# An FFT layer followed by a two-matmul feed-forward layer: the opening's way from B to y is rerouted, and two A units of the second batch move into the step loop

## The chip, the cores and the metric

One kernel on one core of a Trainium2 chip. The metric is the device time of one execution in microseconds; a run's profile gives one execution seen by the hardware profiler. Engines are named as in the profile: PE (TensorE matmul), DVE (VectorE), ACT (ScalarE), POOL (GpSimd), SP (SyncE, which here only issues DMAs).

## The reference

```python
# x: (8, 3008, 256) fp32
X = rfft(x, axis=1)
Yr = Xr @ w_r - Xi @ w_i + b_r
Yi = Xr @ w_i + Xi @ w_r + b_i
Yr, Yi = shrink(Yr, 0.01), shrink(Yi, 0.01)      # sign(v) * max(|v| - lam, 0)
y = irfft(Yr + 1j * Yi, n=3008, axis=1)           # -> 24064 tokens x 256
h = y @ w_in                                      # 256 -> 2048
g = where(h > 0, h, exp(min(h, 0)) - 1)
out = g @ w_out                                   # 2048 -> 256
```

## The kernel before

**The transform.** 3008 = 47 x 64, and each of the 8 batches goes through five kinds of unit:

- A (6 units, `unit_A`): the 64-point transform over x, four sequence columns of 256 at a time; the PSUM result is copied to a bf16 tile `A` (a pair of units fills one tile), which is written to a DRAM scratch `DA`. `load_Z` reads DA back in another partition order.
- X (8 units): the second transform stage, from Z to `XT`.
- M (12 units): multiplication with the weights and the shrinking, from XT to `Y`; bias and K sums on DVE, clip and subtract on POOL.
- B (6 units, `unit_B`, v = 0 to 5): the first inverse stage, two pairs at a time, from Y to `Bz`, which is written to a DRAM scratch `DB`. `load_Bs(b, w)` reads DB back in another partition order: 96 partitions, (k, c, h), each with the eight rows 8w to 8w + 7, for w = 0 to 3, each w a quarter of the batch's output.
- y (8 units, `unit_Y`): the last inverse stage, two units for each w, from `Bs` to the bf16 tile `yT`.

**The feed-forward layer** is a loop of steps (`for i in range(n + LAG)`). A step takes 512 tokens and two of the 16 blocks of 128 hidden channels: `front_mm` (PSUM `hps`, two banks of four), ACT exp to `Et`, a clamp of Et to 0..1 (`Elu.least`, on DVE in steps 0 to 3, afterwards on POOL), DVE `gT` = max(Et - 1, hps), and two steps later `back` (PSUM `ps_o` with `w_out_r`). Eight steps finish 512 tokens. Transform units of later batches are placed into the steps, at most one per step: its matmuls stand between the two halves of `front_mm`, and its PSUM copy comes with `flush()` after the first or second exp.

**Order.** Everything is issued in the order in which the program calls it (a manual schedule). Engines and queues work in order. A planner (`units`) chooses the unit of each step; the string `FIRST` fixes it for the first 33 steps (y: batch 0; X, M, B: batch 1; "-": none).

**The opening**, before the loop, computes batch 0 up to two y units, and the six A units of batch 1 (`ahead=True`). PE is kept busy with dummy matmuls (`idle_pe`, tile `ips`). In its last part the order is: first_M (M of batch 0) interleaved with `fB(0)` to `fB(5)`; `load_Bs(0, 0)` and `(0, 1)`; six A units with `idle_pe(2)` between them; `load_Bs(0, 2)`, `(0, 3)`; `load_w_in(3)`; `load_Z(1, ...)`; y units 0 and 1.

**Weights.** w_in comes in four quarters through staging tiles (`load_w_in`; the first three use the slots of the three Et tiles) and is scaled into `w_in_s` (`scale_w_in`): quarters 0 and 1 on DVE, 2 on ACT, 3 in the step loop on DVE. x of batch 1 and w_out are loaded by POOL's DMA queue behind a small POOL copy (`gate`) that waits for Z of batch 0.

**DMA semaphores.** DMAs from SP and ACT take eight completion semaphores in turn, so a DMA waits until the one eight places earlier has landed.

Lines that the text names (numbers of the profile): L163 A matmuls; L128 and L130 PSUM copies on DVE and ACT; L175 and L177 writes of DA; L186 `load_Z`; L197 X; L214 M of batch 0; L306 Yt, an SBUF-to-SBUF load of later batches; L347 B matmuls; L365, L366 and L368 copies to Bz; L373 writes of DB; L386 `load_Bs`; L397 y; L412 dummy matmuls; L696 `load_w_in`; L779 M4; L788 and L790 `scale_w_in`; L861 front_mm; L878 exp; L883 and L885 the clamp on POOL and DVE; L895 gT; L913 back; L246, L288, L289, L293 POOL's share of M.

Of the kernel before, what the change touches and what calls it, by code (L numbers as in the profile page):

```python
# [8 lines left out]
ALU = mybir.AluOpType  # L9
AF = mybir.ActivationFunctionType  # L10
BF16 = mybir.dt.bfloat16
F32 = mybir.dt.float32
# [13 lines left out]
def kernel(  # L26
# [115 lines left out]
            f()  # L142
        after.clear()

    def unit_A(b, u, alone=False, on_dve=False, ahead=False):
        ci, uu = u // 2, u % 2
        if uu == 0:
            if ahead and ci == 1:
                A_of[b, ci] = xtp.tile([P, 3, 8, D], BF16, name="A", tag="XT")[:, 0]
            elif ahead and ci == 2:  # L150
                A_of[b, ci] = late2.tile([P, 8, D], BF16, name="A", tag="osb")
            elif alone:
                A_of[b, ci] = wk4.tile([P, 8, D], BF16, name="A", tag="Bs")
            else:
                t = "Bz" if b == 2 and ci == 2 else "A"
                A_of[b, ci] = wk2.tile([P, 8, D], BF16, name="A", tag=t)
            if ci == 0:
                DA_of[b] = dram.tile([NJ, P, D], BF16, name="DA", tag="DA")
        xt, A = xts[ci], A_of[b, ci]
        dav = DA_of[b].rearrange("j p d -> p j d")  # L160
        ps = unit_ps("aps", alone or ahead)
        for j in range(2):
            nc.tensor.matmul(  # L163
                ps[:, j, :], lhsT=M1[:],
                rhs=xt[:, 4 * uu + 2 * j : 4 * uu + 2 * j + 2, :], start=True, stop=True,
            )
        def done():
            evac(
                A[:, 4 * uu : 4 * uu + 4, :].rearrange("p n d -> p (n d)"),
                ps[:].rearrange("p a b -> p (a b)"), on_dve,  # L170
            )
            j0 = 8 * ci
            if alone:
                j0 += 4 * uu
                nc.sync.dma_start(dav[:, j0 : j0 + 4, :], A[:, 4 * uu : 4 * uu + 4, :])  # L175
            elif uu == 1:
                nc.sync.dma_start(dav[:, j0 : j0 + 8, :], A[:])  # L177

        later(alone or ahead, done)
# [151 lines left out]
    def unit_B(b, v, alone=False, on_dve=False):  # L331
        if v % 2 == 0:
            t = "A" if alone and v == 4 else "Bz"
            Bz_of[b, v // 2] = wk2.tile([P, 8, D], BF16, name=t, tag=t)
            if v == 0:
                DB_of[b] = dram.tile([K1, P, D], BF16, name="DB", tag="DB")
        Bz = Bz_of[b, v // 2]
        ps = unit_ps("bps", alone)
        psj = ps[:].rearrange("p s (q d) -> p (s q) d", d=D)
        if b < 2:  # L340
            Y = Y_of.pop((b, v))[:]
            if b == 1:
                Y = Y.rearrange("p i c d -> p i (c d)")
            for pp in range(2):
                for c in range(2):
                    for s in range(2):
                        nc.tensor.matmul(  # L347
                            ps[:, s, pp * D : pp * D + D],
                            lhsT=M3f[c][s * N2 : s * N2 + N2, 2 * v + pp, :],
                            rhs=Y[s * N2 : s * N2 + N2, pp, c * D : c * D + D],  # L350
                            start=(c == 0), stop=(c == 1),
                        )
        else:
            Yt = Yt_of.pop((b, v))
            for j in range(4):
                nc.tensor.matmul(  # L356
                    psj[:, j], lhsT=M3[:, 4 * v + j],
                    rhs=Yt[:, j % 2, j // 2 * D : j // 2 * D + D], start=True, stop=True,
                )
        def done():  # L360
            o = 4 * (v % 2)
            Bv = Bz[:, o : o + 4, :].rearrange("p (q s) d -> p s q d", s=2)
            psv = ps[:].rearrange("p s (q d) -> p s q d", d=D)
            if on_dve:
                nc.scalar.copy(Bv[:, :, 0], psv[:, :, 0])  # L365
                nc.vector.tensor_copy(Bv[:, :, 1], psv[:, :, 1])  # L366
            elif b < 2:
                nc.scalar.copy(Bv, psv)  # L368
            else:
                nc.scalar.copy(Bz[:, o : o + 4, :], psj)  # L370
            if alone or (b == 1 and v > 3):
                k0 = 4 * v
                nc.sync.dma_start(  # L373
                    DB_of[b][k0 : k0 + 4].rearrange("k p d -> p k d"), Bz[:, o : o + 4, :]
                )
            elif v % 2:
                k0 = 8 * (v // 2)
                nc.sync.dma_start(DB_of[b][k0 : k0 + 8].rearrange("k p d -> p k d"), Bz[:])

        later(alone, done)  # L380

    def load_Bs(b, w):

        Bs = wk4.tile([4 * K1, 8, D], BF16, name="Bs", tag="Bs")
        dv = DB_of[b].rearrange("k (c h m) d -> (k c h) m d", c=2, h=2)
        nc.sync.dma_start(Bs[:], dv[:, 8 * w : 8 * w + 8, :])  # L386
        Bs_of[b, w] = Bs

    def unit_Y(b, u, alone=False, on_dve=False):
        w, dt = u // 2, u % 2  # L390
# [36 lines left out]
    with tc.tile_pool(name="stagep", bufs=1) as stagep:  # L427
# [66 lines left out]
        for e in range(2):  # L494
# [5 lines left out]
            iota("", None, [[-30, NV]], base=b3, cm=-15, out=m3i[hi])  # L500
            iota("", None, [[-30, NV]], base=b3 + 480, out=m3i[mid_])
            iota("", None, [[2, NV]], base=e, out=k1t[N2 * e : N2 * e + N2])
        n2row = iota("n2row", [P, N2], [[1, N2]])
        arow = iota("arow", [P, N1], [[1, N1]], out=arow_t[:])


# [184 lines left out]
    def load_w_in(q):  # L691
# [4 lines left out]
        nc.sync.dma_start(wf[:], w_in_v[:, :, q * FQ : q * FQ + FQ])  # L696
        w_in_f.append(wf)

    def load_w_out(hh):
        hf = slice(hh * NFT // 2, (hh + 1) * NFT // 2)  # L700
        nc.gpsimd.dma_start(w_out_r[:, hf, :], w_out_v[:, hf, :])
# [15 lines left out]
        unit_B(0, v, alone=True, on_dve=on_dve)  # L717

    load_w_in(0)
    gate(Z_of[0][:, 8, 0:1])  # L720
    for ci in range(3):
        load_x(1, ci)
# [35 lines left out]
    first_M(1, 1, True)  # L758
    first_M(2, 0, False)
    fB(0)  # L760
    load_w_in(1)
    first_M(2, 1, True)
    first_M(3, 0, False)
    fB(1)
# [3 lines left out]
    first_M(4, 1, True)  # L768
    first_M(5, 0, True)
    fB(3)  # L770
    load_w_in(2)
    first_M(5, 1, True)
    let_go()
    fB(4)
    idle_pe(3)
# [2 lines left out]
    for h, w in enumerate((w40, w41)):  # L778
        nc.gpsimd.tensor_scalar(  # L779
            M4v[:, :, h], r4[0 : 2 * NR], w[0 : 2 * NR], None, ALU.mult  # L780
        )
    load_Bs(0, 0)
    load_Bs(0, 1)

    def scale_w_in(q, on_dve, f=slice(0, FQ)):
        dst = w_in_s[:, :, q * FQ + f.start : q * FQ + f.stop]
        if on_dve:
            nc.vector.tensor_scalar_mul(dst, w_in_f[q][:, :, f], 2.0 / S)  # L788
        else:
            nc.scalar.activation(dst, w_in_f[q][:, :, f], AF.Copy, scale=2.0 / S)  # L790

    scale_w_in(0, True)
    for u in range(6):
        unit_A(1, u, on_dve=bool(u % 2), ahead=True)
        if u == 1:
            scale_w_in(1, True)
        idle_pe(2)
    for w in (2, 3):
        load_Bs(0, w)
    load_w_in(3)  # L800
    scale_w_in(2, False)
    for s0, s1 in ((0, 8), (8, NS)):
        load_Z(1, s0, s1)
    idle_pe(3)
    for u in range(2):
        unit_Y(0, u, alone=True, on_dve=bool(u % 2))
    first.close()
# [148 lines left out]
    LB, YB, ZX, LEAD, XW = 6, 7, 6, 52, 2  # L956
    SHUN = ("FFX",)

    FIRST = "yy-yyXXXXXXXXyMMyMMBMMBMMBMMMMBBB"

    def due(b, w):

# [1 line left out]

    def units():

        at = {("A", 1, k): 0 for k in range(6)} | {("y", 0, k): 0 for k in range(2)}
        xat = {(2, c): s for c, s in enumerate((12, 18, 22))}
        xat |= {(3, c): PER + 1 + 3 * c for c in range(3)}
        when = lambda *u: at.get(u, 10 * n)  # L970
# [3 lines left out]
        for t in range(1, n):  # L974
# [33 lines left out]
            if t <= len(FIRST):  # L1008
                kind = FIRST[t - 1]
                b = {"y": 0, "A": 2}.get(kind, 1)  # L1010
                u = None if kind == "-" else (kind, b, count(kind, b))
            elif must:
                u = must
            elif "M" in can and was != "M" and (tight or t % NPAIR != 1):
                u = can["M"]
            elif "B" in can and not (can["B"][1] > 1 and lately[-3:] in SHUN):
                u = can["B"]
            elif "M" in can and tight:
                u = can["M"]
            else:  # L1020
                early = t < 6 or ("y" in can and can["y"][2] < 2)
                u = next((can[k] for k in ("yXA" if early else "XAy") if k in can), None)
# [8 lines left out]
    def plan():  # L1031
# [8 lines left out]
            ):  # L1040
                whole.add((b, k))
        for (kind, b, k), t in at.items():
            if t == 0:
                continue
            name = "Y" if kind == "y" else kind
            f0[t].append(put(name, b, *((k // 2, k % 2) if kind == "M" else (k,))))
            if (kind, k) == ("X", 7):
                for j in range(2):
                    mid[t + 1 + j].append((unit_D, (b, j)))
            if (kind, k) == ("B", 5):  # L1050
                f1[t + (b > 1)] += [(load_Bs, (b, w)) for w in range(4)]
            if (kind, k) == ("A", 5):
                for p in range(2 if b == 2 else 4):
                    w = 8 if p == 0 or b > 2 else 24
                    f1[t + (0, 1, 3)[min(max(b - 2, 0), 2)] * p].append((load_Z, (b, 8 * p, 8 * p + w)))
        for (b, c), t in xat.items():
# [2 lines left out]
            f1[5 + k].append((weight_sum, (k,)))  # L1059
        for c in range(2):  # L1060
            f1[24 + c].append((turn_M3, (c,)))
            f1[4 + c].append((scale_w_in, (3, True, slice(FQ // 2 * c, FQ // 2 * c + FQ // 2))))
        return f0, f1, mid

    NST = 2
# [87 lines left out]
```

## Time and profile before

| | us |
|---|---|
| median of 3 runs | 881.48 (880.74 to 883.64) |
| profiled execution: its time | 882.21 |
| its span, first to last instruction | 880.1 |
| granted TensorE clock, mean | 0.998 |
| first y unit of batch 0 | 56.66 |
| first matmul of step 0 | 58.04 |
| first X unit of batch 1 (step 6) | 70.52 |
| one step with an X or y unit | 2.13 |
| one step with an M unit | 2.45 |

A line of the chain gives start, length and what ran. A line of the timeline gives start, length, engine, line and operation with its tiles, count, and in brackets the idle time before it with what ended it. SPq is SP's issuing of DMAs: the length is that of the issues, not of the transfer. In the DMA view q1 is the hardware queue (issued by SP), q0 the queue of POOL.

### The profile page before, as it was taken

Reading aid. Unit: us, or ns where it says so; the run is one execution under the profiler, and the core shown is the slowest. Engines: PE = TensorE matmul, PEld = TensorE weight load, DVE = VectorE, ACT = ScalarE, POOL = GpSimd, SP = SyncE. Lnnn points to the kernel's source line nnn. Section 1 sums busy time; section 2 is a strip of 40 time slices with the busy share of each in tenths; the row PEclk is TensorE's granted clock in tenths of the full one; section 3 lists DMA queues with packets and bytes.
Section 4 is the critical chain, followed back from the end, with each engine's and each line's share of the span. In section 5 each row is a group of like instructions: output and inputs, shape, how many; then the busy total and the mean of one; then the engine's idle time right before and its main releaser. Section 6 shows DMA issues by size and latency. Waiting matters only on the chain.

```text
span 880.1 us, 20614 instructions
## 1 busy us (share of the span) xinstructions
PE 864.8 (98%) x7850; PEld 707.1 (80%) x7850; DVE 657.0 (75%) x1066; ACT 726.1 (83%) x1217; POOL 651.9 (74%) x981
## 2 busy tenths in 40 slices
PE   8889999999999999999999999999999999999997
PEld 3447888888888888888889888898888988888886
DVE  8767886688777787677876777767776788767775
ACT  6668998899878998899978998789987888786664
POOL 6707995689767887698866888668886699766664
PEclk9999999999999999999999999999999999999999
DMA  8995346643485343643464444553435023331111
GB/s 262 345 268 135 97 122 186 194 146 92 121 247 161 115 126 97 188 141 93 135 178 136 128 124 118 156 168 93 136 112 142 25 67 82 104 100 36 42 33 49
DMA packets 106382, 116.68 MB, mean 133 GB/s; under 512 B 10886, under 2 KB 96012, under 8 KB 103404
## 3 DMA queue, kind: packets, MB, share of 16 engines
q1 hardware_dynamic: 100124, 87.85, 35.8%
q0 software_dynamic: 6016, 27.40, 10.0%
q8 instruction: 61, 1.00, 0.5%
q14 instruction: 37, 0.30, 0.1%
q10 hardware_dynamic: 144, 0.13, 0.0%
HBM read 55.32 MB, written 49.81 MB: 119 GB/s over the span
## 4 chain that ended last, share of the span: by engine, by line
PE 85%; POOL 6%; DVE 4%; DMA 2%; issue 1%; ACT 1%; POOLq 0%; DVEq 0%; SPq 0%
PE ps_o L913 35%; PE hps L861 34%; PE mps L262 5%; PE xps L197 2%; PE aps L163 2%; POOL Et L883 2%; PE yps L397 2%; PE bps L356 1%; POOL Y L293 1%; PE mps L214 1%; DVE gT L895 1%; DMA Z<-DA 1%; DVE yb L279 1%; POOL yb L288 1%; DMA DA<-A 1%
## 5 line engine op out<-in xcount | busy, mean ns | idle before, releaser
L895 DVE SCALAR_TENSOR_TENSOR gT<-Et,hps 128x512 fp32r<-128x512 f32 x752 | 493.4, 683 | 161.8 <-POOL Et L883 160.8
L913 PE MATMUL ps_o<-w_out_r,gT 128*128 128x256 f32 x3008 | 473.9, 300 | 0.1
L883 POOL TENSOR_SCALAR Et<-Et 128x512 f32<-128x512 f32 x576 | 350.4, 616 | 165.7 <-ACT Et L878 164.3
L861 PE MATMUL hps<-yT,w_in_s 128*128 128x64 bf16 (+8 forms) x2833 | 441.2, 281 | 1.7 <-DVE gT L895 0.6
L913 PEld LDWEIGHTS ps_o<-w_out_r,gT 128*128 128x128 f32 x3008 | 400.0, 188 | 46.2 <-DVE gT L895 0.3
L878 ACT ACTIVATE Et<-hps 128x512 f32<-128x512 f32 x584 | 343.7, 605 | 97.1 <-PE hps L861 93.8
L861 PEld LDWEIGHTS <-w_in_s 128*128 128x128 bf16 x2833 | 167.0, 98 | 58.0 <-issue 13.6
L875 ACT ACTIVATE Et<-hps 128x512 f32<-128x512 f32 x168 | 99.5, 592 | 19.1 <-PE hps L861 18.2
L876 ACT ACTIVATE Et<-Et 128x512 f32<-128x512 f32 x168 | 106.1, 632 | 5.3
L293 POOL TENSOR_TENSOR Y<-yb,clip 128x512 bf16<-128x512 f32 x84 | 108.6, 1293 | 0.3
L288 POOL TENSOR_TENSOR yb<-yb,bias_d 128x256 f32<-128x256 f32 x68 | 49.8, 732 | 30.1 <-DVE yb L279 30.0
L289 POOL TENSOR_SCALAR clip<-yb 128x512 f32<-128x512 f32 x84 | 51.6, 614 | 13.4 <-DVE yb L275 7.4
L246 POOL TENSOR_TENSOR Xd<-XT 128x256 bf16<-128x256 bf16 x84 | 56.5, 673 | 0.0
L130 ACT CAST XT<-xps 128x768 bf16<-128x768 f32 x61 | 48.5, 795 | 3.5 <-PE xps L197 3.5
L130 ACT CAST yT<-yps 128x752 bf16<-128x752 f32 x63 | 49.2, 782 | 2.4 <-PE yps L397 2.4
L130 ACT CAST A<-aps 128x1024 bf16<-128x1024 f32 x45 | 45.3, 1009 | 7.2 <-PE aps L163 7.0
L262 PE MATMUL mps<-wsum,XT 128*128 128x256 bf16 x336 | 50.4, 273 | 0.0
L279 DVE TENSOR_TENSOR yb<-mps,Kb 128x512 f32<-128x512 f32 x68 | 47.0, 691 | 2.5
L278 DVE TENSOR_TENSOR Kb<-mps,bias_bc 128x256 f32<-128x256 f32 x68 | 28.7, 422 | 23.6 <-PE mps L262 23.6
L163 PE MATMUL aps<-xt,M 128*128 128x512 f32 x96 | 38.3, 480 | 1.9 <-DMA xt<-in_x_dram 1.1
L397 PEld LDWEIGHTS <-Bs 96*128 96x128 bf16 x512 | 27.8, 98 | 13.6 <-DMA Bs<-DB 2.1
L197 PEld LDWEIGHTS <-Z 96*128 96x128 bf16 x512 | 27.5, 97 | 11.4 <-DMA Z<-DA 2.5
(124 smaller groups left out, 513.2 us busy)
## 6 DMA issues: line engine op xcount, KB each, us to landing
xt<-in_x_dram POOLq DMA_DIRECT2D x21, 1024.0 KB, 5.4
out_dram<-osb SPq DMA_DIRECT2D x158, 128.0 KB
Bs<-DB SPq DMA_DIRECT2D x32, 384.0 KB
DA<-A SPq DMA_DIRECT2D x21, 512.0 KB
DB<-Bz SPq DMA_DIRECT2D x20, 512.0 KB
Z<-DA SPq DMA_DIRECT2D x26, 384.0 KB
Yt<-Y SPq DMA_DIRECT2D x144, 64.0 KB
xt<-in_x_dram POOLq DMA_DIRECT2D x6, 512.0 KB, 6.1
```

Of the source, the lines that this page charges most:

```text
L130: nc.scalar.copy(dst, src)
L246: nc.gpsimd.tensor_tensor(Xd_of[b, k][:], XT[:, :, 0, o : o + P], XT[:, :, 1, o : o + P], ALU.subtract)
L262: nc.tensor.matmul(dst, lhsT=lhs(dt), rhs=rhs(dt), start=dt == 0, stop=dt == 1)
L288: nc.gpsimd.tensor_tensor(yb[:, D : 2 * D], yb[:, D : 2 * D], bias_d[:], ALU.add)
L293: nc.gpsimd.tensor_tensor(Y_, two(yb), two(clips[0]), ALU.subtract)
L861: nc.tensor.matmul(hps[s][:, a:z], lhsT=w_in_s[:, dt, ft * P : ft * P + P], rhs=yT_of[b][:, dt, t0 + a - c0 : t0 + z - c0], start=(dt == 0 ...
L875: nc.scalar.activation(e, h, AF.Relu, scale=-1.0)
L876: nc.scalar.activation(e, e, AF.Exp, scale=-1.0)
L878: nc.scalar.activation(e, h, AF.Exp)
L883: nc.gpsimd.tensor_scalar(e, e, 1.0, 0.0, ALU.min, ALU.max)
L895: nc.vector.scalar_tensor_tensor(g_of[self.i][:, p], self.E[:, p], -1.0, self.h[p], ALU.add, ALU.max)
L913: nc.tensor.matmul(po[q][:, i_ % 2, :], lhsT=gT[:, s, i_ * P : i_ * P + P], rhs=w_out_r[:, ft, :], start=(ft == 0 and i_ % 2 == 0), stop=( ...
```

## The change

1. **Direct loads.** The part of Bs(0, 0) that comes from v = 3, 4, 5 is copied from Bz to Bs inside SBUF: 12 loads of 16 KB, each from 32 partitions (every fourth) to 4. For v = 3 POOL issues four, for v = 4 SP four, for v = 5 ACT two and SP two. Rows of v = 0 to 2 come through DB with `load_Bs(0, 0, 0, 12)`, issued after `fB(3)`. The writes of DB for v = 4, 5 come later (`write_B`), ahead of `load_Bs(0, 1)`.
2. **Row order.** So that a quarter w is every fourth partition of Bz, the order of the 64-point index is permuted (`n2row`), and every `load_Bs`, of all batches, reads eight separate rows of 512 bytes per partition instead of 4 KB in one piece.
3. **v = 5.** Its PSUM result lies in two one-bank tiles, so that ACT's and DVE's copies don't share one.
4. **A units of batch 1.** Units 0 to 3 stay ahead of the loop (the last in two one-bank tiles); unit 4 goes into step 0 (copied by DVE), unit 5 into step 1 (copied by ACT); both write into the buffer that held Bz of v = 4, 5. `load_Z(1, ...)` follows in step 1.
5. **Order of units.** y2 to y6 in steps 2 to 6, X in steps 7 to 14, y7 in 15, M in 16 to 19; from step 20 on as before.
6. **Weights.** w_in quarters 1 and 2 are asked for with quarter 0, ahead of x of batch 1. Quarter 0 is scaled by DVE before `let_go`, 1 and 2 by POOL.

```diff
-        ps = unit_ps("aps", alone or ahead)
+        if apart:
+            two = [pre1.tile([P, 512], F32, name="aps", tag="mps1")[:] for _ in range(2)]
+        else:
+            ps = unit_ps("aps", alone or ahead)
+            two = [ps[:, j, :] for j in range(2)]
...
+                evac(dst, ps[:].rearrange("p a b -> p (a b)"), on_dve or (b, u) == (1, 4))
...
             if on_dve:
-                nc.scalar.copy(Bv[:, :, 0], psv[:, :, 0])
-                nc.vector.tensor_copy(Bv[:, :, 1], psv[:, :, 1])
+                for s, copy, eng in ((0, nc.scalar.copy, nc.scalar), (1, nc.vector.tensor_copy, nc.sync)):
+                    copy(Bz[:, o + 2 * s : o + 2 * s + 2, :].rearrange("p q d -> p (q d)"), out_[s])
+                    for q in range(2):
+                        direct(b, v, 2 * s + q, eng, 2 * q + s)
...
+            if alone and v in (3, 4):
+                for j in range(4):
+                    direct(b, v, j, (nc.gpsimd, nc.sync)[v - 3])
+            if alone and v > 3:
+                return
...
+    def direct(b, v, j, eng, k=None):
+        if (b, 0) not in Bs_of:
+            Bs_of[b, 0] = wk4.tile([4 * K1, 8, D], BF16, name="Bs", tag="Bs")
+        src = Bz_of[b, v // 2][:, 4 * (v % 2) + j, :].rearrange("(p w) d -> p w d", w=4)
+        k = 4 * v + (j if k is None else k)
+        eng.dma_start(Bs_of[b, 0][4 * k : 4 * k + 4], src[:, 0, :])
+
+    def write_B(v):
+        dst = DB_of[0][4 * v : 4 * v + 4]
+        o = 4 * (v % 2)
+        if v == 5:
+            for s in range(2):
+                nc.sync.dma_start(
+                    dst[s:4:2].rearrange("q p d -> p q d"), Bz_of[0, 2][:, o + 2 * s : o + 2 * s + 2, :]
+                )
+        else:
+            nc.sync.dma_start(dst.rearrange("k p d -> p k d"), Bz_of[0, 2][:, o : o + 4, :])
+
+    def load_Bs(b, w, k0=0, k1=K1):
+        if (b, w) not in Bs_of:
+            Bs_of[b, w] = wk4.tile([4 * K1, 8, D], BF16, name="Bs", tag="Bs")
+        dv = DB_of[b].rearrange("k (g m w) d -> (k g) m w d", g=4, w=4)
+        nc.sync.dma_start(Bs_of[b, w][4 * k0 : 4 * k1], dv[4 * k0 : 4 * k1, :, w, :])
-    def load_Bs(b, w):
-        Bs = wk4.tile([4 * K1, 8, D], BF16, name="Bs", tag="Bs")
-        dv = DB_of[b].rearrange("k (c h m) d -> (k c h) m d", c=2, h=2)
-        nc.sync.dma_start(Bs[:], dv[:, 8 * w : 8 * w + 8, :])
-        Bs_of[b, w] = Bs
...
-        n2row = iota("n2row", [P, N2], [[1, N2]])
+        n2row = iota("n2row", [P, N2], [[NS, 2], [1, 8], [8, 4]])
...
     load_w_in(0)
+    load_w_in(1)
+    load_w_in(2)
...
     fB(0)
-    load_w_in(1)
...
     fB(3)
-    load_w_in(2)
+    load_Bs(0, 0, 0, 12)
     first_M(5, 1, True)
+    scale_w_in(0, nc.vector)
     let_go()
     fB(4)
     idle_pe(3)
     fB(5, True)
...
-    load_Bs(0, 0)
-    load_Bs(0, 1)
-    scale_w_in(0, True)
-    for u in range(6):
-        unit_A(1, u, on_dve=bool(u % 2), ahead=True)
+    for v in (4, 5):
+        write_B(v)
+    for q in (1, 2):
+        scale_w_in(q, nc.gpsimd)
+    for u in range(4):
+        unit_A(1, u, on_dve=bool(u % 2), ahead=True, apart=u == 3)
         if u == 1:
-            scale_w_in(1, True)
+            load_Bs(0, 1)
         idle_pe(2)
     for w in (2, 3):
         load_Bs(0, w)
     load_w_in(3)
-    scale_w_in(2, False)
-    for s0, s1 in ((0, 8), (8, NS)):
-        load_Z(1, s0, s1)
-    idle_pe(3)
     for u in range(2):
         unit_Y(0, u, alone=True, on_dve=bool(u % 2))
...
-    FIRST = "yy-yyXXXXXXXXyMMyMMBMMBMMBMMMMBBB"
+    FIRST = "ayyyyyXXXXXXXXyMMMMBMMBMMBMMMMBBB"
...
-        at = {("A", 1, k): 0 for k in range(6)} | {("y", 0, k): 0 for k in range(2)}
+        at = {("A", 1, k): 0 for k in range(5)} | {("y", 0, k): 0 for k in range(2)}
```

## The prediction

> **What bounds the kernel now.** All times are us from the start of the profiled span. First the page's busy shares: PE has no room after the opening, so only the opening can give time.
>
> ```profile
> PE 864.8 (98%) x7850; PEld 707.1 (80%) x7850; DVE 657.0 (75%) x1066; ACT 726.1 (83%) x1217; POOL 651.9 (74%) x981
> ```
>
> Then the chain that ended last, in order of time, 0 to 150:
>
> ```profile
> 47.08 0.61 PE bps L347 x8
> ...
> 53.95 1.24 DVE A L128
> 55.25 6.85 DMA DA<-A
> 62.30 8.18 DMA Z<-DA
> 70.52 0.52 PE xps L197 x8
> 71.47 0.94 PE ps_o L913 x8
> 73.63 0.91 PE ps_o L913 x8
> ```
>
> After 71.47 every link is PE, 2.13 a step. Before it the end hangs on batch 1: last A copy (55.18), write of DA, load of Z, first X unit in step 6. The timeline of 40 to 72 shows a second path close beside it:
>
> ```profile
> 47.44 1.98 SPq L373 DMA_DIRECT2D DB<-A  x2
> 52.39 0.80 SPq L386 DMA_DIRECT2D Bs<-DB  x2
> 53.28 4.56 SPq L177 DMA_DIRECT2D DA<-A  x3
> 56.66 0.84 PE L397 MATMUL yps<-M,Bs 96*128 96x94 bf16 x16 [1.65 <-DMA Bs<-DB]
> 70.52 0.52 PE L197 MATMUL xps<-M,Z 96*128 96x96 bf16 x8 [0.53 <-DMA Z<-DA]
> ```
>
> Last B matmul at 47.68, writes of DB issued until 49.4, landed and reloaded from 52.39, first y unit at 56.66: 9 us of detour through DRAM, which A units and idle matmuls fill without shortening it. X0 then waits only 0.53. So both paths must get shorter; shortening one alone gives little.
>
> **Part 1: when can y0 start?** It needs all 12 direct loads and the partial load of the first 12 rows of DB.
>
> The partial load stands on SP behind the write of v=3 (Bz copied at 45.78) and waits until the writes of v=0 to 2 have landed. Those are late for a reason seen in the DMA view of 38 to 40:
>
> ```profile
> DMA packets 697, 0.70 MB, mean 349 GB/s; under 512 B 16, under 2 KB 697, under 8 KB 697
> q0 software_dynamic: 697, 0.70, 186.6%
> ```
>
> The write issued at 37.69 gets no packet here: POOL's queue (x of batch 1, then w_out) has all engines; the hardware queue first moves in 41.5 to 42 and has moved 0.79 MB (v=0 and a w_in quarter) by about 44.8, v=2 by about 46.5. The change asks for both w_in quarters (1.05 MB) at 23, beside x. At the 422 GB/s of 28 to 30, w_out ends 2.5 us later and the writes start near 44.2 instead of 41.7, but 0.52 MB less stands before them. Estimate for v=2 landed: 47.9 (47.0 to 48.6).
>
> SP then issues the partial load (0.4) and, in order behind it, six direct loads. The trace has one kind of SBUF-to-SBUF load:
>
> ```profile
> L306 SPq DMA_DIRECT2D Yt<-Y x144: 461/590/1734, 193.8 to 756.9; - x144
> ```
>
> A write of DB costs 0.36. The loads are a quarter of a Yt load, so I take 0.46 each, 0.36 to 0.59: 48.3 + 6 x 0.46 = 51.1. From an issue to use: first packets come 1.0 after the issue of Bs at 52.39, PE starts 0.4 after the last packet of Bs, 16 KB itself is little; 1.9 in all. y0 at 53.0 (52.3 to 54.3). ACT's two loads go out from 48.3 and POOL's four from 45.8 at 0.62 to 0.99 each (its rows for x and w_out) and land 2.7 later (its 128 KB store), so by 52.5: not last. PE itself reaches y0 at 52.3: four A units from 47.68, the third after the DVE copy (1.23) of the second. Gain at y0: 56.66 - 53.0 = **3.7**.
>
> The Trainium skill ("DMA: Bandwidth & Descriptors", "Why a DMA increments its semaphore by 16 and not by 1") says that a load is spread over the largest number of DMA engines up to 16 which divides the leading dimension on both sides, so here 4 of 16, and from SP and ACT always the same four. By that, eight 16 KB loads put 64 packets on each of four engines, about 1.5 us at the 1383 packets in 2 us of 58 to 60; spread over 3 us of issues it adds some 0.2, an estimate that would make the sum below -2.9; nothing in this trace shows such a load.
>
> **Part 2: steps 0 to 6, counted from y0.** Before: least on DVE at +2.93, step 3 at +6.64, step 4 at +8.48 (65.14), step 7 at +15.59 (72.25).
> - A(1,4) and A(1,5) leave idle time and enter steps 0, 1: 2 x 0.47 of PE, now on the path. A(1,4)'s DVE copy (1.23) goes ahead of the Et clamp of step 0: behind it are all clamps and gT (0.75 + 1.28 a step) of steps 0 to 3, and PE needs gT of step i to refill hps in step i+2. The less finely cut matmuls of step 0 give 0.3 back. A(1,5)'s ACT copy (1.01) stands between the two exps of step 1. Tracing copies, exps and PSUM releases through gives first gT at +4.6 (was +3.77), step 2 at +5.2, step 3 at +7.35, step 4 at +9.5: 1.0 later.
> - The A copies also wait until the direct loads and the writes of DB for v=4, 5 have left Bz's old buffer. Those are issued behind the last direct load, 52.3, and land 2.7 to 3.3 later (49.08 to 52.39 before), about y0 + 2.2. The copy is due at y0 + 2.6: covered by 0.4. Without that cover DVE stalls by the difference, and PE from step 2.
> - Steps 4 to 6 all carry a y: 3 x 2.13, so step 7 at +15.9. Before, step 6 held 0.73 of waiting for Z, which falls out if Z is on time.
> Step 7: 53.0 + 15.9 = 68.9 against 72.25: **-3.35**.
>
> **Part 3: Z.** A(1,5)'s copy ends at y0 + 5.4 = 58.4 instead of 55.18. SP's DA write for the third tile follows. Queued ahead of it since 52: 0.52 MB DB, 1.05 DA, 1.17 Bs, 0.52 w_in. At 345 GB/s for 512-byte writes (57 to 61) and 250 to 347 for the reads it is through at 62.7 to 64.2; landing 0.9; then Z. Batch 0's Z took 4.67 from issue (18.89) to first X (23.56). So Z is there at 68.5 to 69.8; X0 is due at 69.3. The second Z load, 1.15 MB at 250 GB/s, is due at 73.6 and there at 73 to 74.7. I put +0.25 on this (0 to 1.1).
>
> Bs is now read in 512-byte pieces instead of 4 KB. No read row has that size; 1 KB reads of w_out ran at 349, 4 KB reads of Bs at 267, 512-byte writes at 347. I take no loss; at half of 267 the three loads would add 4.4 to the queue. Later batches: Bs(1) is issued at 137.95 and its first y runs at 145.4, so 3 us of slack hide it.
>
> **Part 4: edits that cost nothing.** DVE's w_in scaling (0.68) fits a 0.94 wait for ACT at 45.6. POOL's two scalings (512 elements cost 0.60 as a cast, so 1.2 each) run at 50 to 53 where POOL was idle from 45.0 to 66.5; ACT's exps of steps 1 and 2 wait for them at about 56.7 and 59. Splitting the v=5 copy starts DVE 0.6 sooner, but its loads stand behind SP anyway. The order M M M M in steps 16 to 19 instead of M M y M M leaves POOL (0.61 + 0.67 + 1.29, in half of them 0.73 more, so about 2.9 of work per M step of 2.45) some 1 us more behind; before, four Ms at steps 27 to 30 passed without a PE gap. From step 20 the order is the same, and the gain stays.
>
> **Sum.** -3.35 + 0.25 = -3.1. The profiled execution took 882.21 (span 880.1, 2.1 around it): 879.1; it stands 0.73 above the median of 881.48, so **878.4**. Differences below 0.3% (2.6 us) can't be told from none.
>
> **Rivals.**
> 1. *More gain.* Writes land at 47.0, issues cost 0.36: y0 at 52.3 where PE is ready, Z hidden, the ramp 0.5 better: -4.5, 877.0. For: all bounds come from rows. Against: they must hold together.
> 2. *Z takes the end (slower).* If A copy to X0 takes the 15.3 it took before, X0 of step 7 comes at 58.4 + 15.3 = 73.7 against 72.69 for that step's X before: +1.0, 882.5. It decides once the stretch exceeds 11.0. Against: before, two more DA writes and all Bs loads lay in that stretch. For: slow 512-byte reads would put 4.4 into it.
> 3. *POOL's scaling is slow.* The timeline has it once:
>
> ```profile
> 20.35 0.60 POOL L634 CAST wcat_r<-w_i_f 128x512 bf16<-128x512 f32 x1
> 20.93 3.09 POOL L635 TENSOR_SCALAR wcat_s<-w_i_f 128x512 bf16<-128x512 f32 x1
> ```
>
> At 3.09 per 512 the two scalings end at 56.2 and 62.4, and exp of step 2 waits from 59.0: +3.4, so 881.8. Against: at 20.93 DVE ran L581, L672 and L726 with two SBUF inputs; at 50 to 53 it copies from PSUM. The Trainium skill ("SBUF — State Buffer", "Who interferes with whom") says just that: a DVE instruction with two SBUF inputs blocks a GpSimd one that reads SBUF. By that rule, and the trace agrees with its one 3.09 row, this rival falls away.
> 4. *SP's issues are dear.* At the 1.73 maximum of the Yt row the six end at 58.7, y0 at 60.6: +4.3, 885.8. It costs time from 1.1 an issue up.
>
> **Numbers.** Forecast with its own spread of 0.9 either way 0.52 (three quarters beyond 2.6), rival 1 0.17, rival 2 0.15, rival 3 0.08, rival 4 0.08. Faster 0.39 + 0.17 = 0.56. Same 0.13 + 0.11 of rival 2 + 0.05 of rival 3 = 0.29. Slower 0.04 + 0.03 + 0.08 = 0.15. The range runs from rival 1's end, 876.8, to rival 2's, 882.6.
>
> **What would show it.** First yps at 52.3 to 54.3, waiting for direct loads; six SP issues of 0.36 to 0.59 from about 48.3; DVE's A copy at y0 + 2.6 without a DMA wait; step 4 about 1.0 later against y0 than now; xps of X0 near 69.3 with less than 1 of waiting; equal steps from 20 on. Wrong if yps starts after 56, if exps wait for POOL, or if X0 comes after 72.7.

## The result and the profile after

| | before | changed |
|---|---|---|
| median of runs | 881.1 us (880.44 to 883.64, 6 runs) | 884.9 us (884.49 to 886.95, 6 runs) |
| ratio | 1 | 1.0040, 95% interval 1.0026 to 1.0053 |
| profiled execution | 882.21, span 880.1 | 886.21, span 884.2 |

The change costs 0.4%, where a gain of 3.1 us was forecast. The profiled execution of the changed kernel is one of its longer ones; the account below goes by the two traces, which stand 4.0 apart, and the ratio decides.

The page's busy shares hardly move, so the opening is again the place to look:

```profile
PE 866.8 (98%) x7833; PEld 708.4 (80%) x7833; DVE 656.1 (74%) x1066; ACT 725.6 (82%) x1216; POOL 659.6 (75%) x987
```

The chain that ended last, in order of time (start, length, what):

```profile
47.49 0.58 ACT A L377
48.09 2.11 DMA Bs<-A
50.22 1.02 ACT A L130
...
54.02 0.54 SPq L406
...
54.61 2.24 DMA DB<-A
56.85 1.41 PE yps L434 x16
...
76.05 0.34 PE xps L203 x8
```

Batch 1's write of DA and its Z are off this chain. In their place stands SP, issuing direct loads (L406), and y0 starts where it did: 56.84 instead of 56.66. (The link just ahead of y0 is the write of v=4, which y0 does not read. The profile infers a link from the semaphore that came last; this write is the next DMA behind the last direct load.) SP's own timeline shows why, and what came behind:

```profile
50.10 0.71 SPq L424 DMA_DIRECT2D Bs<-DB  x1
50.90 3.66 SPq L406 DMA_DIRECT2D Bs<-A  x6
54.61 0.44 SPq L417 DMA_DIRECT2D DB<-A  x1
55.16 0.98 SPq L413 DMA_DIRECT2D DB<-A  x2
...
58.03 0.61 SPq L424 DMA_DIRECT2D Bs<-DB  x1
...
62.17 1.06 SPq L733 DMA_DIRECT2D w_in_f<-in_moe_w_in_dram  x1
...
70.54 0.80 SPq L192 DMA_DIRECT2D Z<-DA  x2
```

The partial load waits until 50.10, six direct loads take 0.61 each behind it, and other transfers are queued behind those: the writes of DB for v=4 and 5 go out at 54.61 instead of 47.44, the second Bs load at 58.03 instead of just after 52.4, the fourth w_in quarter at 62.17 instead of 60.11. Z goes out at 70.54 instead of 62.30 for another reason: it waits for the write of DA issued at 64.84, right behind the copy of A(1,5) in step 1 (63.81 to 64.82).

PE, with fewer A units and fewer idle matmuls to run, now rests 4.40 ahead of y0. The windows view (us; then busy time and instructions of PE, PEld, DVE, ACT, POOL; granted TensorE clock; DMA share; GB/s) shows what follows:

```profile
52.00:54.00 2.00, 0.44 (x2) 0.00 (x0) 1.09 (x2) 0.14 (x1) 2.00 (x2) 1.00 0.31 83
54.00:56.00 2.00, 0.00 (x0) 0.00 (x0) 0.00 (x0) 0.00 (x0) 0.78 (x1) 0.73 0.26 76
58.00:60.00 2.00, 0.96 (x8) 0.64 (x5) 0.94 (x1) 0.45 (x1) 0.00 (x0) 0.50 0.75 221
64.00:66.00 2.00, 2.00 (x16) 1.08 (x13) 1.34 (x4) 1.83 (x4) 0.00 (x0) 0.71 1.19 222
```

The granted clock falls to 0.50 (at 54.92) and is back only after 65; the first 16 y matmuls take 1.41 instead of 0.84.

Where the 4.0 us arise can be read from the starts of the second-layer matmuls (ps_o), one group of eight a step; group 4 runs in step 6. The table gives, for every kernel of this study, y0 and some of these starts against the kernel before, each from one profiled execution (which can lie a microsecond, in f1 and e2 nearly two, from its kernel's median), and beside it the ratio of the timed runs. M units stand in steps 15 to 30, between groups 12 and 26.

| kernel | y0 | group 0 | 3 | 4 | 6 | 12 | 26 | ratio (95%) |
|---|---|---|---|---|---|---|---|---|
| changed | +0.18 | +3.64 | +3.93 | +3.23 | +3.20 | +3.21 | +4.07 | 1.0040 (1.0026 to 1.0053) |
| c1 | -0.28 | +0.93 | +1.19 | +1.39 | +2.60 | +2.69 | +3.48 | 1.0052 (1.0040 to 1.0065) |
| c2 | -0.83 | +1.96 | +2.25 | +1.54 | +1.52 | +1.52 | +2.33 | 1.0029 (1.0018 to 1.0041) |
| c3 | -1.56 | +0.54 | +0.83 | +0.12 | +0.09 | +0.48 | +1.27 | 1.0022 (1.0013 to 1.0032) |
| c4 | +0.32 | +3.05 | +3.34 | +3.89 | +4.39 | +4.42 | +4.42 | 1.0055 (1.0042 to 1.0068) |
| d1 | -0.24 | +2.30 | +3.37 | +3.57 | +3.90 | +3.90 | +3.90 | 1.0041 (1.0027 to 1.0054) |
| d2 | -0.80 | -0.58 | -0.58 | +0.79 | +2.39 | +2.39 | +2.39 | 1.0027 (1.0016 to 1.0037) |
| d3 | -0.86 | +3.23 | +3.41 | +2.71 | +2.69 | +2.69 | +2.69 | 1.0023 (1.0013 to 1.0033) |
| d4 | -0.38 | +1.20 | +1.17 | +0.47 | +0.45 | +0.45 | +0.39 | 1.0004 (0.9995 to 1.0014) |
| e1 | +1.49 | +2.79 | +2.77 | +2.33 | +2.34 | +2.34 | +2.34 | 1.0028 (1.0018 to 1.0037) |
| e2 | -0.60 | +0.47 | +0.47 | -0.23 | -0.08 | -0.08 | -0.13 | 1.0024 (1.0015 to 1.0034) |
| e3 | -0.34 | -0.34 | -0.40 | +0.61 | +0.61 | +0.61 | +0.62 | 1.0015 (1.0006 to 1.0024) |
| f1 | -0.27 | +6.71 | +7.62 | +6.92 | +6.89 | +6.89 | +6.84 | 1.0061 (1.0045 to 1.0078) |
| f2 | +0.21 | +1.97 | +2.30 | +1.59 | +2.16 | +2.88 | +3.68 | 1.0036 (1.0024 to 1.0048) |
| f3 | -2.05 | -0.80 | -0.51 | -1.22 | -1.24 | -1.24 | -0.37 | 0.9999 (0.9985 to 1.0014) |
| g3 | -2.48 | -1.15 | -0.86 | -1.56 | -1.59 | -1.58 | -0.82 | 1.0003 (0.9993 to 1.0012) |

For the changed kernel: +0.18 at y0, +3.75 from there to group 3, then -0.73 because the kernel before lost that much waiting for Z in step 6, +0.86 in the M units, together 4.06; the steps up to group 30 give 0.06 back.

### The profile page after: what moved, and what is told of

Same layout as the page of the kernel before. It is cut to its first block, busy times and chain, and to the rows that moved or that the text cites. A ratio compares the mean times of both kernels' runs of the same rounds, so it can differ in the third digit from the quotient of the medians.

```text
span 884.2 us, 20618 instructions
## 1 busy us (share of the span) xinstructions
PE 866.8 (98%) x7833; PEld 708.4 (80%) x7833; DVE 656.1 (74%) x1066; ACT 725.6 (82%) x1216; POOL 659.6 (75%) x987
## 4 chain that ended last, share of the span: by engine, by line
PE 85%; POOL 6%; DVE 5%; DMA 1%; issue 1%; ACT 1%; SPq 0%; POOLq 0%; DVEq 0%
PE ps_o L949 35%; PE hps L897 35%; PE mps L268 5%; PE xps L203 2%; PE aps L167 2%; PE yps L434 2%; POOL Et L919 2%; PE bps L367 1%; POOL Y L299 1%; PE mps L220 1%; DVE gT L931 1%; DVE yb L285 1%; POOL yb L294 1%; PE bps L358 1%; DMA xt<-in_x_dram 1%
## 5 line engine op out<-in xcount | busy, mean ns | idle before, releaser
L897 PE MATMUL hps<-yT,w_in_s 128*128 128x512 bf16 (+8 forms) x2823 | 443.2, 282 | 1.5 <-DVE yT L128 1.0
L434 PE MATMUL yps<-M,Bs 96*128 96x94 bf16 x512 | 32.4, 208 | 4.5 <-DMA DB<-A 4.4
```

What stands on the lines that cost most here:

```text
L434: nc.tensor.matmul(psv[:, j, 0 : 2 * N1], lhsT=Bs[:, j, dt * P : dt * P + P], rhs=M4[:], start=True, stop=True,)
L897: nc.tensor.matmul(hps[s][:, a:z], lhsT=w_in_s[:, dt, ft * P : ft * P + P], rhs=yT_of[b][:, dt, t0 + a - c0 : t0 + z - c0], start=(dt == 0 ...
```

## The experiments

### Is it the clock? (c1, d4)

c1 adds idle matmuls where PE rests; d4 takes them away from the kernel before.

```
c1:  load_w_in(3)
   + idle_pe(18)
     for u in range(2): unit_Y(0, u, ...)
d4 (kernel before), in the loop over the six A units:
   - idle_pe(2)
   + idle_pe(2 if u < 3 else 0)
     ...
   - idle_pe(3)          # ahead of y0
```

> The changed kernel with 18 more idle matmuls (0.22 us each, 4.0 us) in the 4.40 us that PE waits for y0; everything else as it is. Theory 1 (the wait lets the granted clock fall to 0.50 until 65, and that is most of the loss): the granted clock stays near 1.00 from 52 to 66, y0 stays at about 56.8, step 7 starts at about y0 + 15.9 = 72.7 instead of 75.45, the time is 2.7 less than the changed kernel's, about 882.2, ratio to the kernel before about 1.001. Rival (the loss is the two A units' own chain: DVE's copy ahead of the clamps, exps behind the copies): the clock is up but step 7 stays near 75 and the time within 0.8 of 884.9.

Measured: 886.65 us, ratio 1.0052. The windows view and two waits of c1 (the DVE timeline, then PE's):

```profile
58.00:60.00 2.00, 1.76 (x10) 1.10 (x11) 0.77 (x2) 0.79 (x2) 0.00 (x0) 1.00 0.76 207
```

```profile
69.51 1.34 DVE L739 TENSOR_SCALAR w_in_s<-w_in_f 128x512 bf16<-128x512 f32 x1 [1.15 <-DMA w_in_f<-in_moe_w_in_dram]
```

```profile
75.25 0.52 PE L203 MATMUL xps<-M,Z 96*128 96x96 bf16 x8 [0.71 <-DMA Z<-DA]
```

The clock is 1.00 and group 3 is 2.74 earlier than in the changed kernel. But then DVE waits for the fourth w_in quarter before it can do the next gT, PE waits for Z, and most of it is gone by group 6. Theory 1 is right on the clock and wrong on the time: a second path, transfers asked for late, stands 0.5 us behind the first in these traces (+2.69 instead of +3.21 at group 12), and the timed runs show no gain. What stays of the stretch from y0 to group 3 at full clock is +1.47 (1.19 + 0.28), so the clock's share of the 3.75 is 2.28. That is the share in the traced execution, whose mean granted clock is 0.992; the other five have 0.995 or 0.996 and so lose less to it.

> The kernel before with 9 of its idle matmuls taken out between the last A units and y0; nothing else changed. Theory (a wait of PE of some 2.5 us and more lets the granted clock fall to 0.5 for some 7 us): PE rests 2.7 to 3.5 ahead of y0 at 56.7, the clock is 0.50 to 0.75 from 56 to 63, step 7 comes 1.0 to 2.5 later, time 882.5 to 884. Rival (the fall of the clock came from something else, such as the loads or the order of units): clock 1.00, time within 0.8 of the kernel before.

Measured: 881.94 us, ratio 1.0004. PE rested 2.31, and the clock fell to 0.50 until after 62:

```profile
56.28 1.43 PE L397 MATMUL yps<-M,Bs 96*128 96x94 bf16 x16 [2.31 <-DMA Bs<-DB]
```

```profile
58.00:60.00 2.00, 1.80 (x12) 0.77 (x12) 0.69 (x2) 0.60 (x1) 0.00 (x0) 0.50 1.15 347
```

So the rest alone brings the clock down; nothing of the change is needed for it. It costs 1.20 at group 0, but 0.70 of that is waiting for Z that step 6 had anyway, and 0.4 reaches the end: less than was expected of it.

### When can y0 start? (c3, c2)

```
c3:  fB(3)
   - load_Bs(0, 0, 0, 12)
     ...
     fB(4)
   + load_Bs(0, 0, 0, 12)
c2:  load_w_in(1) back behind fB(0), load_w_in(2) back behind fB(3)
```

> The changed kernel with the partial load of Bs asked for on SP behind the four direct loads of v=4 instead of ahead of them. Theory 3 (the six direct loads cost 0.61 each on SP and wait 2 to 3 us behind a load that waits for DB): the four go out from about 47.8 to 50.2, then the partial load, then the two of v=5, the last issued near 52 instead of 54.5, y0 at 54 to 54.6 instead of 56.84, so 2.3 off the wait, and with the shorter fall of the clock 2.3 to 4 off the time: 881 to 882.6. Rival (the landing of the partial load or of POOL's direct loads is last anyway): y0 after 56 and a time within 1 of 884.9.

Measured: 883.44 us, ratio 1.0022, the best of the first four. SP's timeline of c3:

```profile
47.49 2.55 SPq L406 DMA_DIRECT2D Bs<-A  x4
50.08 0.64 SPq L424 DMA_DIRECT2D Bs<-DB  x1
50.82 1.20 SPq L406 DMA_DIRECT2D Bs<-A  x2
```

Four direct loads fit into the time that SP had waited, and y0 comes at 55.10, 1.74 earlier than in the changed kernel, for 1.6 us of time (0.0018 of 881.8). It is 0.5 later than expected, since y0 follows the end of the last issue by 3.1, not 2.0 to 2.6. The theory holds: SP's order was what kept y0.

> The changed kernel with the requests for w_in quarters 1 and 2 back behind B units 0 and 3. Theory 2 (the early requests keep x and w_out on the DMA engines 2.5 to 4 us longer, so the writes of DB land late): w_out ends near 43.5 again, the writes of v=0 to 2 land by about 47, the partial load goes out at 47 to 48 instead of 50.10, y0 comes at 54.3 to 55.3 instead of 56.84, the time falls by 2 to 3.5 (part of it because the wait and with it the fall of the clock get shorter), to about 882. Rival (the third quarter then stands ahead of the partial load on SP and its 0.52 MB ahead of it in the hardware queue): y0 at 56 to 57 and no gain, 884 to 885.

Measured: 884.15 us, ratio 1.0029. The partial load goes out at 49.01 instead of 50.10 and y0 comes at 55.83, half the expected step. The early requests do delay the writes of DB, by 1.1, not by the 2 to 3 that the theory gave.

### Four M units in a row (c4, g3)

```
c4: - FIRST = "ayyyyyXXXXXXXXyMMMMBMMBMMBMMMMBBB"
    + FIRST = "ayyyyXXXXXXXXyMMyMMBMMBMMBMMMMBBB"
g3 (on f3, below): both osb copies of the second block on ACT
```

> The changed kernel with the order of units in steps 1 to 18 as before it: y in 2 to 5, X from 6, then y M M y M M, so that the four M units in a row are gone. Theory 4 (four M units in a row with the osb copy on DVE among them cost 0.8 to 1.0 in steps 17 to 26): the steps from 20 on come 0.8 to 1.0 earlier, time about 884.0, if X0, one step earlier at 73.3, finds Z. Rival (Z, issued at 70.54, needs 4.7 and comes at 75.2): PE waits up to 1.9 for X0 and the time is 884.9 to 885.9.

Measured: 886.44 us, ratio 1.0055. Both halves came true: X0 waits 1.08 for Z, and later X another 0.30, which takes the time up; and from group 12 to 26 nothing is lost. In the table every kernel with the new order loses 0.76 to 0.87 there (changed, c1, c2, c3, f2, f3, g3), every one with the old order 0.01 at most. The chain of the changed kernel at the fourth M:

```profile
101.47 0.61 DVE Kb L278
102.10 0.70 DVE yb L281
102.94 0.81 PE mps L268 x6
```

> f3 with both osb copies of the second block (step 16) on ACT, so that DVE has 0.68 less among the four M units in a row. Theory (four M units in a row overbook DVE: two adds per M, two gT per step and the copy, and hps is refilled late; steps 16 to 26 of f3 lose 0.87): 0.4 to 0.7 of that comes back, the steps from 26 on stand 0.8 to 1.1 ahead of the kernel before in the trace, time 0.4 to 0.7 under f3's, ratio to the kernel before 0.9990 to 0.9995. Rival (POOL, which clamps and subtracts for each M, is what is late, or ACT's exps are held by the second copy): steps 16 to 26 lose 0.8 or more again and the ratio is 0.9997 to 1.0005.

Measured: 882.41 us, ratio 1.0003; groups 12 to 26 lose 0.76, against 0.87 in f3. The copy is not what is late, so the rival holds as far as that. Whether DVE's adds or POOL's clamps and subtractions behind them set the pace stays open. So does why the same four in steps 27 to 30 lose nothing in the changed kernel (+4.07 at group 26, +4.01 at group 30).

### All A units ahead again (d1, d2, d3, e1, e2)

These keep the direct loads, put the six A units back ahead of y0 and the units back into the old order, and then take one late transfer after another off the queue.

```
d1:  for u in range(6): unit_A(1, u, ..., ahead=True); load_Z(1, ...) ahead of the loop
     FIRST = "yy-yyXXXXXXXXyMMyMMBMMBMMBMMMMBBB"; idle_pe(8) ahead of y0
d2 = d1 with  direct(b, v, j, nc.gpsimd if v == 3 or j < 2 else nc.sync)
     and load_Bs(0, 0, 0, 12) behind fB(5)
d3 = d2 with  load_w_in(3) right behind that load; load_Bs(0, 3) behind load_Z(1, 0, 8)
e1 = d2 with  write_B(4); load_w_in(3) right behind fB(4); idle_pe(2) ahead of y0
e2 = e1 with  load_Bs(0, 3) behind load_Z(1, 0, 8)
```

> The changed kernel with the direct loads, the early w_in requests and the POOL scalings kept, but all six A units of batch 1 ahead of y0 again, the order of units in steps 1 to 33 and the load of Z as in the kernel before, and 8 more idle matmuls so that PE does not rest ahead of y0. Theory (direct loads as issued gain nothing at y0; the loss is the fall of the clock, the two A units in the loop with the later Z behind them, and the four M units in a row): y0 at 56.4 to 57, clock near 1.00, X0 at about y0 + 13.9 = 70.5, the time within 0.8 of the kernel before, about 881.5. Rival (512-byte reads of Bs or the early w_in requests cost by themselves): Z comes later than 72 and the time is 883 to 885.

Measured: 885.79 us, ratio 1.0041. Neither holds, though y0 comes as forecast (56.42). The loss has a new place, the second pair of y units, in PE's timeline:

```profile
62.01 0.51 PE L434 MATMUL yps<-M,Bs 96*128 96x94 bf16 x8 [2.24 <-DMA Bs<-DB]
```

In the old order y2 runs in step 1 and needs the second Bs load. That load waits on SP for the writes of v=4 and 5, which stand behind the direct loads. The detour through DRAM is still there for w=1 to 3, only later. The rest of 2.24 brings the clock down to 0.50 again.

> As d1, with the direct loads issued faster: two of v=4's four on POOL, and the partial load of Bs behind SP's other four instead of ahead of them. Theory (the end at y0 was SP's row of six loads of 0.61 behind a wait): SP is through at about 50.5 instead of 54.5, y0 at 53.0 to 54.5; then Z is the bound (its chain starts at the A copies, which are no earlier than before): X0 waits 2 to 3, starts at 69.5 to 70.5, and the time is 880.5 to 881.5, no or hardly any gain. Rival (Z follows y0 because the reads in front of it are earlier too): X0 at y0 + 13.5, time 878.5 to 879.5.

Measured: 883.8 us, ratio 1.0027. y0 is earlier (55.86, now set by PE's own work) and group 3 is 0.58 ahead of the kernel before. Then all is lost at one place:

```profile
69.54 0.70 DVE L739 TENSOR_SCALAR w_in_s<-w_in_f 128x512 bf16<-128x512 f32 x1 [2.81 <-DMA w_in_f<-in_moe_w_in_dram]
```

The fourth quarter, issued at 60.75, takes 8.77 to land. Z, which was to be the bound, is not waited for.

> As d2, with the fourth w_in quarter asked for right behind the partial load (into the 50 to 56 in which DMA is nearly empty), and the fourth Bs load behind the first load of Z instead of ahead of it, so 0.9 MB less stands ahead of Z. Theory: Z is there 2 to 3 us earlier, X0 at 67 to 68.5 with little wait, step 7 at about 69.5, the time about 878.8 (878 to 880), faster than both kernels. Rival (Z's time is set by the write of DA and its landing, not by what is queued ahead): X0 near 70 and 880.5 to 881.5.

Measured: 884.24 us, ratio 1.0023. With the quarter ahead of the writes of DB, the writes land at 57.9, and y2 waits 3.00 for the second Bs load. Both expectations miss.

> As d2 (A units ahead, old order, POOL takes two of v=4's direct loads), but SP asks for the write of v=4 and for the fourth w_in quarter right behind v=4's two direct loads at about 48.5, while DMA is nearly empty, and only 2 idle matmuls stand ahead of y0. Theory (what was left of d2's loss was DVE waiting in step 4 for the fourth quarter, asked for at 60.75 behind everything; and Z is the bound behind it): no gT wait in steps 4 and 5, y0 at 53.6 to 54.6, X0 at 68 to 69.5, time 879.5 to 880.8, faster than both kernels by 0.1 to 0.2 per cent. Rival (0.52 MB at 49 stands in front of the partial load, or Z's own time is fixed by the writes of DA): y0 after 55 or X0 at 70 to 71, time 881 to 882.

> As e1, with the fourth Bs load asked for behind the first load of Z. Theory (Z is last in step 6, and each 0.39 MB ahead of it costs about 1.2): X0 1 or so earlier than in e1 where that waits for Z, time up to 1 lower. Rival: SP waits for DA at the first load of Z until 61 to 62, and the fourth Bs lands after 65, so that y6 in step 5 waits 0.5 to 2 and the time is that of e1 or more.

Measured: 884.4 and 884.12 us, ratios 1.0028 and 1.0024. DVE's wait for the quarter is gone, as expected, but y0 waits 1.56 and 1.64 and y2 1.51 and 1.27 for loads, so the rival on y0 is the nearer one (y0 58.15 in e1, 56.06 in e2). In e1's profiled execution B units, writes and A units all ran about 2 us later (the third A unit at 52.24, in e2 at 50.07), so it can't be laid beside e2's step by step. The reason is the clock, which in this execution of e1 was 0.50 from 27.17 to 34.00, in batch 0's transform; f1's traced execution has the same from 26.41 to 33.23.

### The new order of rows by itself (e3)

```
e3 (kernel before): only the 512-byte form of load_Bs, and n2row in its new order
```

> The kernel before with only the new order of rows in Bs, so that every load of Bs reads 512-byte pieces in place of 4 KB; no direct loads, nothing moved. Theory (four times 8 times as many packets cost SP 0.25 to 0.5 more per load and DMA nothing that the end sees): y0 within 0.4 of 56.66, X0 within 0.4 of 70.52, steps from 7 on and in later batches unchanged, ratio within 0.001 of 1. Rival (the small reads are half as fast and push w_in quarter 3 and Z): X0 1.5 to 4 later, ratio 1.002 to 1.004.

Measured: 883.02 us, ratio 1.0015 (1.0006 to 1.0024): between the two. y0 is no later, Z is not waited for, but DVE waits for the fourth w_in quarter in step 4, 2.52 where the kernel before has 0.39:

```profile
69.49 0.43 DVE L788 TENSOR_SCALAR w_in_s<-w_in_f 128x512 bf16<-128x512 f32 x1 [2.52 <-DMA w_in_f<-in_moe_w_in_dram]
```

A Bs load now costs SP 0.64 at the median instead of 0.39. The quarter is asked for 0.44 later than before (60.55) and is there 1.80 later; how much of the rest the small reads ahead of it took is not separated. That is 1.3 us (0.5 to 2.1) from an edit that the prediction put at nothing. It is not a share of the changed kernel's loss that could be subtracted: there everything runs later, and DVE starts on the quarter at 70.93 without a wait.

### The fourth quarter asked for sooner (f2, f3, f1)

```
f2 = c1 with load_w_in(3) right behind write_B(4), write_B(5)
f3 = c3 with load_w_in(3) right behind write_B(4), write_B(5); idle_pe(8) ahead of y0
f1 = d2 with all four load_w_in at the start; load_w_out(1) only behind POOL's direct loads
```

> c1 (the changed kernel with 18 idle matmuls ahead of y0) with the fourth w_in quarter asked for right behind the writes of DB, at about 55.8 instead of 61.6. Theory (curing the clock gained nothing since DVE then waits for the fourth quarter in steps 4 and 5 and PE for Z in step 7, both late behind SP's row): the gT wait of 0.76 and the DVE wait before it go, Z comes up to 1.7 earlier, step 7 on is 1.0 to 1.9 earlier than in c1, time 884.7 to 885.6 with the same 881.8 for the kernel before. Rival (Z alone sets it and does not move): time as c1, 886.2 to 887.

Measured: 885.87 us, ratio 1.0036 where c1 has 1.0052: 1.4 us, with intervals that overlap a little. DVE's wait for the quarter is gone; PE still waits for Z, 0.43 at X0 and 0.69 two X units later. The theory's direction holds, and Z is the wall behind.

> The changed kernel with the partial load behind v=4's direct loads (as c3), 8 more idle matmuls ahead of y0 and the fourth w_in quarter asked for behind the writes of DB at about 53.8. Theory (the three causes add: SP's row, the fall of the clock, the fourth quarter and Z): y0 at 55, clock 1.00, step 3 0.5 to 0.8 ahead of the kernel before, X0 in step 7 at about 71.0 to 71.8, then 0.8 lost in the four M units: time 881.3 to 882.5. Rival (Z is as late as in c3, where it was issued at 68.85 and there by 73): PE waits 1 to 2 for X0 and the time is that of c3, 883 to 883.8.

Measured: 882.58 us, ratio 0.9999. PE's first y unit and DVE's scaling in f3:

```profile
54.61 0.83 PE L434 MATMUL yps<-M,Bs 96*128 96x94 bf16 x16 [0.46 <-DMA DB<-A]
```

```profile
66.50 0.42 DVE L739 TENSOR_SCALAR w_in_s<-w_in_f 128x512 bf16<-128x512 f32 x1
```

The three causes add as expected: with SP's order mended, the rest of PE filled and the quarter on time, X0 waits for nothing, groups 4 to 12 stand 1.2 ahead of the kernel before, and the four M units take 0.87 of that. The whole loss of the change is gone, but no measurable gain is there; g3, above, is the same within what can be told. No kernel of this study was faster than the one before.

> As d2 (A units ahead, old order, direct loads on POOL and SP, partial load behind them), but all four w_in quarters are asked for at 23 and the second half of w_out (1.05 MB) only behind POOL's direct loads at about 50.5, where DMA is nearly empty. Theory (w_out on POOL's queue is what keeps the writes of DB waiting until 47 and the fourth quarter is what DVE waits for in step 4): POOL's queue is through at about 44, the writes of v=0 to 2 land by 46.5, y0 at 53.5 to 55, no gT wait in steps 4 and 5, X0 at 68.5 to 70, time 880 to 881.5, at or under the kernel before. Rival (w_out at 50 to 54 holds back the writes of DB and DA as it did at 38, so the second Bs load and Z come later): y2 waits 1 to 2, X0 after 71, time 883 to 884.5.

Measured: 888.13 us, ratio 1.0061. The rival holds, and worse than it said: with half of w_out issued on POOL's queue at 52.11, the writes of DB for v=4 and 5, issued from 52.37 on, land so late that the second Bs load goes out at 61.54, and y2 waits 5.44.

## Why the prediction was wrong, step by step

Step 7 was to start at 68.9 and started at 75.45. Of these 6.55, 3.84 arise before y0 and 2.71 between y0 and step 7. The M units add another 0.86 (groups 12 to 26).

**Part 1, the term that failed first.** y0 was to come at 53.0 and came at 56.84. Four terms of that sum were too small, each the same way. The writes of v=0 to 2 had landed by 50.1, not 47.9 and outside the stated 47.0 to 48.6; c2 puts 1.1 of this down to the early w_in requests, and the rest stays open. The partial load's own issue took 0.8 with the gap behind it, not 0.4. A direct load's issue costs 0.61, not 0.46, just over the upper bound; the rows of the direct loads:

```profile
L406 SPq DMA_DIRECT2D Bs<-A x6: 542/543/652, 50.9 to 54.0; - x6
L406 POOL DMA_DIRECT2D Bs<-Bz x4: 587/593/692, 45.9 to 47.7; - x4
```

And y0 follows the last issue by 2.3, in c3 by 3.1, not 1.9. The row that bounded the issue was a load four times the size; a direct load is hardly cheaper to issue (0.54 against 0.59 at the median, without the gap). The mechanism, direct loads in order behind a load that waits, was seen, and c3 shows that turning the two round was worth 1.6 us.

That the hardware queue gets next to nothing while POOL's runs was read rightly from the trace of before, but how long was not: in 44 to 45 POOL's queue still moves 380 packets, where it moved 9 before. The DMA view of 38 to 40 in the changed kernel:

```profile
q0 software_dynamic: 455, 0.72, 132.5%
q1 hardware_dynamic: 8, 0.01, 1.5%
```

The Trainium skill ("DMA: Bandwidth & Descriptors", "Queues, rings and completion order") says that an engine goes round between the queues that have work, a packet at a time. 8 packets beside 455 do not look like that, and for this stretch the measurement decides. From 41 to 44 the same trace does look like it, with 525 packets of q1 beside 705 of q0, and so does f1 in 57 to 59, with 395 beside 440. Whether SP's packets were ready before 41, the traces do not tell.

**What stood behind SP was not counted.** The prediction followed the moved step to y0 and to Z, but not the others on SP's queue. The writes of v=4 and 5, 7 us later, hold the second Bs load (d1, d3, e1, e2, f1: waits of 1.3 to 5.4 at y2), and the fourth w_in quarter holds DVE's gT (c1, d2). Rival 4 had the right queue, with a price of 1.73 an issue that was never paid; 0.61 was enough together with the wait in front.

**Part 2.** From y0 to step 7 was to take 15.9 and took 18.6. The two A units cost about what was forecast: of the 1.47 left at full clock, 0.5 is the first hps matmul waiting for DVE's copy of yT (1.04 idle instead of 0.54, also in d1 to d3, where no A unit is in the loop), so about 1.0 is theirs, as predicted. What was missing is the clock, 2.28. The prediction took idle matmuls out of the sum as work that costs nothing, without asking what they were for. By its own sum PE would have rested only from 52.3 to 53.0; the rest of 4.40 follows from the miss of Part 1. The Trainium skill ("TensorE: Matmul & The Clock Gate", "HAM oscillation — how this bites in real kernels") warns of PE rests above some 3.4 us. Here 4.40 brought the clock to 0.50, but so did 2.31 (d4), 2.37 (c3), 2.24 (d1) and even 1.54 (in e1, ahead of an X unit of batch 0 at 26.13), while 1.65 (before) and 1.64 (e2) left it at 1.00. So the measurement differs, and the length of one rest does not decide.

The traces show a finer pattern. In the first 100 us of each, every change of the granted clock lies a whole number of windows of 3.41 us from the last one, and the falls go by how long PE was busy within such a window. Where the clock never fell, the windows are counted on from its first change, at 6.13 in the kernel before. The first two rows are from e1, the others from the kernel before; PE's busy time is the number behind the comma, the granted clock the third from the right:

```profile
23.76:27.17 3.41, 1.70 (x27) 1.33 (x28) 3.36 (x5) 2.24 (x4) 3.41 (x6) 1.00 1.02 266
27.17:30.58 3.41, 2.95 (x25) 1.85 (x23) 2.13 (x3) 1.64 (x3) 1.86 (x3) 0.50 1.09 408
53.92:57.33 3.41, 1.76 (x21) 0.96 (x20) 1.23 (x1) 0.98 (x2) 0.00 (x0) 1.00 0.94 274
57.33:60.75 3.42, 2.58 (x28) 1.31 (x25) 2.03 (x4) 2.45 (x5) 0.00 (x0) 1.00 1.15 345
```

1.70 was followed by a fall and 1.76 was not. In the 17 traces all eleven windows with a busy share of 0.50 or less (0.94 of 3.42 in the changed kernel, up to 54.92) were followed by 0.50 in the next, and none with 0.52 or more was. The clock came back behind the first window with 0.88 or more; behind those with up to 0.87 it stayed low. The kernel before thus stood just above the edge.

**Part 3.** Z came late enough to hold PE only where the clock was mended (c1 0.71, f2 0.43) or X0 was put a step earlier (c4 1.08). From the end of A(1,5)'s copy to Z the forecast of 10.1 to 11.4 was about right: in c4, where X0 waited for Z, it took 9.8 (64.59 to 74.41). But the stretch started late, at 64.82 in the changed kernel instead of 58.4. That reading Bs in 512-byte pieces costs nothing failed too: 1.3 us in e3, where DVE waited for the w_in quarter, which the sum had put behind Bs on the queue and then forgotten.

**Part 4.** POOL's scalings took 2.75 each, not 1.2; the second took as long as the first although DVE rested through its last 1.7. They were hidden all the same: they ended at 54.8, before any exp needed them (the first starts at 60.36). Rival 3's price, 3.09 per 512 elements, was not paid (1.38). The four M units in a row were to be free and cost 0.8.

**The rivals.** Rival 2 was to end on the other side by Z; it did not in the changed kernel, since SP and the clock held PE longer, but c1 and f2 found it right behind. That both paths must shorten together was said in the first part of the prediction, and the sum then counted on the second with 0.25. (By the prediction's own terms rival 4 costs time from about 1.0 an issue up, not 1.1, and the range's ends, 876.8 and 882.6, stand beside 877.0 and 882.5 in the rivals; the miss does not hang on either.)

## What to carry to other kernels

A transfer that is split into many small ones is paid by the queue that issues them: count every later entry of that queue, to the one that ends last, not only the transfer that was split. An engine's filling work has a use until the trace shows that it has none; take it out only with the granted clock in view, and look at PE's busy share in every few microseconds, not only at its longest rest. And where two paths end within half a microsecond of each other, mending the one on the chain buys nothing until the second is priced too.

## What was not expected of the hardware

- The granted clock fell to 0.50 behind windows of 3.41 us in which PE was busy for 0.50 or less, whether it rested for 4.97 us (c4) or for 1.54 and 0.17 (e1). In the changed kernel it stayed there for three windows, from 54.92 to 65.16, 8.3 us after PE had work again.
- A direct load of 16 KB from SBUF to SBUF costs SP 0.54 and a gap of 0.05; two cost ACT 1.73 (in c3 1.91) of its own time; POOL's four land 3.7 to 4.9 after their issue in the changed kernel, 2.7 to 4.0 in c3.
- POOL's scaling from 128x1024 f32 to bf16 took 2.75, with DVE copying from PSUM beside it or at rest, 1.38 per 512 elements against 0.60 for a cast.
